# Cosine attention with a highway layer on one core: the k rows of batch 4 are transposed by DMA, and the order of the work is written anew

## The chip, the cores and the metric

The kernel runs on one core of a Trainium2 chip. The metric is the device time of one execution in microseconds (us); less is better. Five engines run side by side, each through its own list of instructions in order: TensorE (PE in the profile, with its weight loads as PEld), VectorE (DVE), ScalarE (ACT), GpSimd (POOL) and SyncE (SP). SP computes nothing; it issues DMAs. POOL and ACT issue some too.

## The reference

Eight batches of twelve heads, 448 rows of 64 numbers. Attention uses normalised q and k, so its scores are cosines; a highway layer follows over the 3584 rows of 768.

```python
q_n = q / (norm(q) + 1e-06)
k_n = k / (norm(k) + 1e-06)
attn = softmax(q_n @ k_n.T / tau)
x = (attn @ v) as rows of 12 * 64            # 3584 x 768
H = maximum(x @ w_h, 0)
T = 1 / (1 + exp(-(x @ w_t + b_t)))
out = T * H + (1 - T) * x
```

q, k, v are 8 x 12 x 448 x 64 float32, w_h and w_t 768 x 768. Products are taken in fp16 with float32 sums.

## The kernel before

**Work and tiles.** Each batch has three groups of four heads; a "group" below is such a set, named by batch and number (4 0 is the first of batch 4). For each group, q and k are loaded (SP loads q, POOL loads k and v), squared on ACT or POOL, summed over 64 columns on DVE (line 439), and turned into a scale by a reciprocal root: Ln and Exp on ACT for batch 0 and a part of batch 1 (lines 465 and 468), seven small DVE steps for later ones (lines 450 to 457). Line 480 multiplies a half of the group by its scale, on POOL or DVE, into the tile qn or kn. Then the group has to be transposed, so that the head's 64 columns lie on the partitions: `turn` (line 484).

**Two ways to transpose.** Either PE does it in seven 128x128 matmuls against an identity (line 496), and DVE copies the result from PSUM to the tile qT or kT (line 499); or one DMA issued by SP does it (line 489). The ranges QDMA and KDMA (line 270) say from which batch on the DMA is used: q from batch 3, k from batch 5. The attention output x is turned by DMA from batch 1 on (line 695, tile xT).

**Scores, softmax, output.** PE multiplies kT and qT (line 506; four matmuls on quarters of the array make two PSUM tiles), ACT takes the exponential (line 538 into E, line 549 into Et for the tail of 64 rows), PE multiplies with v (lines 566 and 574, 65 columns: the 65th gives the row sum), and DVE divides (lines 581 and 582) into x. The highway layer follows per 128 rows: PE (lines 715 and 712; three matmuls make half a sum), DVE adds the bias and takes the products (744, 753, 759, 780), ACT the tanh (757), POOL or DVE the last sum (786), SP stores (793, 796).

**What sets the order.** Nothing is scheduled at run time. `Plan` collects some 1,840 operations, and the table ORDER lists them in the order in which they are put into the engines' lists. SLOTS says which buffer each takes (three kn, three qn, four kT and four qT, eight PSUM banks). ELSEWHERE moves single operations to another engine. BEHIND adds a wait of one operation for another. An engine runs its list in order, so an operation that waits holds up all that stands behind it on its engine. SP's list holds the loads of q, the DMA transposes and the stores in one line. At the start PE runs 43 matmuls on zeros (lines 350 and 354) ahead of and between the first real work.

Of the kernel before, what the change touches and what calls it, by code (L numbers as in the profile page):

```python
# [90 lines left out]
""".split()  # L91
)
SLOTS = {
    "qr": "01010101",
    "kr": "0120121",
    "kn": "012012012012012201021201",
    "vr": "01010110",
    "vp": "01010101",
    "sq": "012012020102102102102102102020202120210102102012",
    "n2": "01010101",  # L100
    "y": "01201201",
    "tu": "01010101010",
# [789 lines left out]
```

## Time and profile before

| | |
|---|---|
| median of three timed runs | 247.79 us (247.62 to 248.25) |
| the profiled execution: its own time | 246.7 us |
| the profiled execution: from first to last instruction (span) | 244.9 us |
| mean granted TensorE clock | 0.991 |
| PE transposes of kn (line 496) | 105 matmuls, 8.3 us busy |
| DMA transposes into kT and qT | 9 and 15 |
| DMA transposes into xT | 28 |

A profile row names a source line, an engine, an operation and the tiles it writes and reads (`out<-in`). A row of the timeline begins with its start and its length in us; in brackets stands the idle time before it and what ended that. Matmuls overlap: one row's length is longer than the distance to the next row's start, and it is the distance that says what an instruction costs on a busy PE. The rows that matter are quoted in the prediction.

### The profile page before, as it was taken

To read this page: it belongs to the slowest core of one execution; us is meant where nothing else is said; L and a number is where in the kernel's file an instruction comes from. 1 tells how busy PE (TensorE), PEld (TensorE's weight loads), DVE (VectorE), ACT (ScalarE), POOL (GpSimd) and SP (SyncE) were. 2 spreads that over 40 slices of the span, in tenths; PEclk is the share of its full clock that TensorE was granted. 3 is DMA by queue.
4 is the path that set the end of the run, shared out by engine and by line. 5 is a ranking of instruction groups with operands and counts; after the bars stand their busy time and mean duration, and the time that the engine had idled before them with its cause. 6 is when DMAs were issued, how large, how long until landed. Compare 5 with 4: busy or idle time off the path is not lost.

```text
span 244.9 us, 8269 instructions
## 1 busy us (share of the span) xinstructions
PE 231.5 (94%) x3304; PEld 143.0 (58%) x3304; DVE 217.4 (89%) x480; ACT 206.3 (84%) x415; POOL 157.9 (64%) x187
## 2 busy tenths in 40 slices
PE   7868899999989999999999999999999999999990
PEld 2334676565765657656664576656565656666550
DVE  4879999999998999999999999899988695768993
ACT  3589999999999999999999999998879787972220
POOL 8596969979983989887676957785665020023340
PEclk9999999999999999999999999999999999999996
DMA  6999999999899969999999899899997647546636
GB/s 224 331 204 265 247 285 225 201 270 226 145 144 235 232 162 230 156 220 220 287 159 202 147 210 212 162 245 197 179 192 156 112 84 148 149 130 130 189 95 155
DMA packets 74647, 47.54 MB, mean 194 GB/s; under 512 B 50288, under 2 KB 71408, under 8 KB 74608
## 3 DMA queue, kind: packets, MB, share of 16 engines
q1 hardware_dynamic: 53776, 32.65, 59.8%
q0 software_dynamic: 19856, 12.68, 39.4%
q10 hardware_dynamic: 976, 1.67, 2.1%
q8 instruction: 26, 0.43, 0.7%
q14 instruction: 13, 0.11, 0.1%
HBM read 38.34 MB, written 11.01 MB: 201 GB/s over the span
## 4 chain that ended last, share of the span: by engine, by line
PE 72%; DVE 10%; ACT 7%; DMA 7%; issue 2%; SPq 1%; DVEq 0%; ACTq 0%
PE B L715 36%; PE B L506 13%; PE B L566 12%; PE B L712 5%; DMA qr<-in_q_dram 4%; ACT E L538 4%; PE B L574 3%; DMA xT<-x 2%; DVE n L439 2%; PE B L496 2%; ACT sq L429 1%; DVE z L744 1%; DVE hm L753 1%; ACT Et L549 1%; DVE qT L499 1%
## 5 line engine op out<-in xcount | busy, mean ns | idle before, releaser
L538 ACT ACTIVATE E<-B 128x448 f16<-128x448 f32 x276 | 135.0, 603 | 9.0 <-PE B L506 6.7
L715 PEld LDWEIGHTS <-xT 128*128 128x128 f16 x576 | 51.2, 98 | 38.7 <-issue 9.6
L786 POOL TENSOR_TENSOR os<-x,hm 128x384 f32<-128x384 f16 x41 | 37.0, 911 | 53.5 <-DVE hm L780 17.4
L715 PE MATMUL B<-wh,xT 128*128 128x384 f16 x288 | 57.2, 326 | 1.0 <-DMA xT<-x 1.0
L715 PE MATMUL B<-wt,xT 128*128 128x384 f16 x288 | 56.3, 326 | 0.1
L439 DVE TENSOR_REDUCE n<-sq 128x14 f32<-128x896 f32 (+1 forms) x50 | 51.0, 1037 | 1.9 <-ACT sq L429 1.7
L506 PE MATMUL B<-qT,kT 64*64 64x448 f16 (+2 forms) x728 | 47.9, 338 | 1.4 <-ACT E L538 0.6
L566 PEld LDWEIGHTS <-E 128*128 128x128 f16 x828 | 38.2, 97 | 10.4 <-issue 5.6
L566 PE MATMUL B<-vp,E 128*128 128x65 f16 x828 | 43.3, 194 | 0.1
L757 ACT ACTIVATE tt<-z 128x768 f16<-128x768 f32 (+1 forms) x32 | 25.9, 810 | 15.5 <-DVE z L744 15.5
L566 PE MATMUL B<-vp,Et 128*128 128x65 f16 x276 | 38.5, 191 | 0.0
L480 POOL TENSOR_TENSOR qn<-qr,y 128x448 f16<-128x448 f32 x38 | 35.0, 935 | 4.5 <-DVE kn L480 1.4
L480 POOL TENSOR_TENSOR kn<-kr,y 128x448 f16<-128x448 f16 x34 | 31.6, 936 | 7.6 <-DVE y L457 2.4
L753 DVE SCALAR_TENSOR_TENSOR hm<-B,x 128x384 f16<-128x384 f32 x53 | 29.0, 551 | 3.9 <-PE B L715 3.5
L744 DVE TENSOR_TENSOR z<-B,bias 128x384 f32<-128x384 f32 x48 | 25.6, 550 | 4.6 <-PE B L715 4.0
L506 PEld LDWEIGHTS <-kT 64*64 64x64 f16 x728 | 17.1, 105 | 20.4 <-issue 15.4
L582 DVE SCALAR_TENSOR_TENSOR x<-B,rd 128x448 f16<-128x448 f32 x46 | 28.0, 617 | 0.7
L566 PEld LDWEIGHTS <-Et 128*128 128x128 f16 x276 | 27.2, 99 | 0.0
L549 ACT ACTIVATE Et<-B 128x448 f16<-128x448 f32 x46 | 26.5, 604 | 0.0
L429 ACT ACTIVATE sq<-qr 128x896 f32<-128x896 f32 (+1 forms) x22 | 22.4, 1018 | 4.6 <-DMA qr<-in_q_dram 4.6
L386 POOL DMA_DIRECT2D vr<-in_v_dram x32 | 22.2, 698 | 5.4 <-DVE vp L511 3.5
L780 DVE TENSOR_TENSOR hm<-tt,hm 128x768 f16<-128x768 f16 (+1 forms) x30 | 15.0, 501 | 0.2
(74 smaller groups left out, 274.4 us busy)
## 6 DMA issues: line engine op xcount, KB each, us to landing
qr<-in_q_dram SPq DMA_DIRECT2D x24, 448.0 KB, 6.8
out_dram<-os SPq DMA_DIRECT2D x47, 192.0 KB, 3.7
kr<-in_k_dram POOLq DMA_DIRECT2D x7, 672.0 KB, 13.8
vr<-in_v_dram POOLq DMA_DIRECT2D x16, 192.0 KB, 10.7
vr<-in_v_dram POOLq DMA_DIRECT2D x16, 144.0 KB, 6.1
out_dram<-os SPq DMA_DIRECT2D x15, 96.0 KB, 3.2
E<-in_k_dram ACTq DMA_DIRECT2D x3, 448.0 KB, 7.5
wt<-in_moe_w_t_dram POOLq DMA_DIRECT2D x1, 1152.0 KB, 23.7
```

The costliest lines, as they stand in the source:

```text
L439: nc.vector.reduce_sum(R("n2", b)[:, c : c + 7 * n], a, axis=AX.X)
L480: ENG[eng].tensor_mul(R(nm + "n", i)[:, :, t, :], source(nm, b, g)[:, t].rearrange("l (j d) -> l j d", d=D), R("y", b)[:, c : c + NJ].unsq ...
L506: nc.tensor.matmul(out[t][64 * h : 64 * h + 64, o[t] : o[t] + w], lhsT=K[ln, j, S_, :], rhs=Q[ln, :, S_, :], start=True, stop=True)
L538: nc.scalar.activation(R("E", n)[:, at : at + 7, :].rearrange("l j x -> l (j x)"), R("B", ("S", n, c, t))[:, 0:S], AF.Exp, scale=1.0 / tau)
L549: op("ACT", f"expt {i} {t}", lambda t=t: nc.scalar.activation(R("Et", (i, t)).rearrange("l j x -> l (j x)"), R("B", ("St", i, t))[:, 0:S], ...
L566: nc.tensor.matmul(U[:, 2 * c + t, :], lhsT=lt.rearrange("l j x -> l (j x)"), rhs=vp[:, 3 * t + m if m < NC else 6 + t, 0:65], start=(m == ...
L582: op("DVE", f"ev {n}", lambda: nc.vector.scalar_tensor_tensor(out=R("x", b)[:, :, D * p : D * p + D], in0=U_()[:, :, 0:D], scalar=0.0, in1 ...
L715: nc.tensor.matmul(P[:, 0:MH], lhsT=xT[:, cc, :], rhs=w_[:, cc, MH * mh : MH * mh + MH], start=(cc == 0), stop=(cc == CC - 1))
L744: op("DVE", f"za {g} {mh}", lambda at=at, sl=sl: nc.vector.tensor_add(R("z", g)[:, sl], R("B", at)[:, 0:MH], biast[:, :] if tail else bias ...
L753: op("DVE", f"hm {g} {mh}", lambda at=at, sl=sl, mh=mh: nc.vector.scalar_tensor_tensor(out=R("hm", g)[:, sl], in0=R("B", at)[:, 0:MH], sca ...
L757: op("ACT", f"th{nb} {g}", lambda: nc.scalar.activation(R("tt", g)[:, 0:W], R("z", g)[:, 0:W], AF.Tanh, scale=0.5), r=[("z", g), ("t0",)], ...
L786: op(e, f"out {g} {mh}", lambda sl=sl, mh=mh, e=e: ENG[e].tensor_add(R("os", g)[:, sl], xpart(mh), R("hm", g)[:, sl]), r=[("gg", g), xk], ...
```

## The change

The one line of logic is the range KDMA. The other four tables (ORDER, SLOTS, BEHIND, ELSEWHERE) are replaced by new ones of the same kind. Three copies and three turns (21 matmuls and their weight loads) leave, three DMA transposes come. Line numbers after the tables are two higher.

```diff
@@ ORDER, SLOTS, BEHIND: other numbers throughout
-1 49 50 4 2 36 51 52 27 57 10 0 53 40 56 7 293 3 30 296 13 24 19 58 32 16 22 55 8 35 300 25 62 64 29 526 5 65 38 66 11
+1 49 50 4 3 42 51 52 30 57 16 0 53 6 56 11 28 296 5 54 18 32 58 26 20 55 9 27 21 526 62 47 25 64 17 63 59 14 293 68 65
...
@@ ELSEWHERE (some of the rows that the text speaks of)
-    "sq1 q 0 0 0": "DVE",
     "sq1 q 0 0 1": "ACT",
-    "sq2 q 0 1 0": "POOL",
-    "qn7 0 0 1": "DVE",
+    "qn7 0 0 0": "POOL",
     "kn7 0 0 0": "POOL",
+    "kn7 0 0 1": "DVE",
-    "kn7 4 0 0": "DVE",
+    "kn7 4 1 0": "DVE",
...
@@ tile_cosine_attention__then__highway_ffn_kernel
-    XDMA, QDMA, KDMA = range(1, B), range(3, B), range(5, B)
+    XDMA, QDMA, KDMA = range(1, B), range(3, B), range(4, B)
```

Three places are shown as the lists of the engines have them. The first is PE's list before, in batch 3's scores, where group 4 2 was turned (kn0 holds its k; seven pairs of line 496, three pairs of line 715 on either side, of which one each is shown):

```order
L715 LDWEIGHTS xT5_113
L715 MATMUL B7_132<-wt_135,xT5_113 128x384
...
L496 LDWEIGHTS kn0_66
L496 MATMUL B1_126<-ident_133,kn0_66 128x128
...
L715 LDWEIGHTS xT2_110
L715 MATMUL B3_128<-wh_134,xT2_110 128x384
```

The same layer of the same rows in PE's list now (xT4 holds what xT5 held before):

```order
L717 LDWEIGHTS xT4_112
L717 MATMUL B6_131<-wt_135,xT4_112 128x384
...
L508 LDWEIGHTS kT2_92
L508 MATMUL B2_127<-qT2_88,kT2_92 64x448
```

No turn stands between the layer and batch 3's next scores any more; the same holds for groups 4 0 and 4 1. Ahead of the first scores of batch 4 PE's list has the same operations as before, less two of the three turns.

The second place is SP's list around batch 4's transposes. Before (q of groups 4 1, 4 0 and 4 2, in this order, go to qT1, qT3 and qT2; `out` rows are stores, `qr` rows loads of batch 6):

```order
L796 DMA out_0_dram<-os0_121 64x768 x2
L489 DMA_TRANSPOSE qT1_87<-qn2_85 128x7x128
L489 DMA_TRANSPOSE qT3_89<-qn1_84 128x7x128
L796 DMA out_0_dram<-os3_124 64x768 x2
L793 DMA out_0_dram<-os1_122 64x384 x2
L373 DMA qr0_61<-in_q_dram 128x2x448
L489 DMA_TRANSPOSE qT2_88<-qn0_83 128x7x128
```

Now (k of groups 4 1, 4 0 and 4 2 goes to kT3, kT0 and kT1; q of groups 4 0, 4 2 and 4 1 to qT3, qT0 and qT1):

```order
L798 DMA out_0_dram<-os0_121 64x768 x2
L491 DMA_TRANSPOSE kT3_93<-kn0_66 128x7x128
L798 DMA out_0_dram<-os1_122 64x768 x2
L491 DMA_TRANSPOSE kT0_90<-kn1_67 128x7x128
L697 DMA_TRANSPOSE xT5_113<-x3_107 128x3x128
L491 DMA_TRANSPOSE qT3_89<-qn2_85 128x7x128
L491 DMA_TRANSPOSE qT0_86<-qn0_83 128x7x128
L375 DMA qr0_61<-in_q_dram 128x2x448
L491 DMA_TRANSPOSE kT1_91<-kn2_68 128x7x128
L795 DMA out_0_dram<-os3_124 64x384 x2
L375 DMA qr0_61<-in_q_dram 128x2x448 x2
L491 DMA_TRANSPOSE qT1_87<-qn1_84 128x7x128
```

The three k transposes stand among those of q, the transpose into qT3 (group 4 0, which is used first) has two k transposes and one of x close ahead of it, and q of group 4 1 went from the first place to the last.

The third place is the start of ACT's list: squares of q and k (line 429), Ln and Exp of the scale (465, 468), and the first exponentials (538). Before, from the first scale on:

```order
L468 ACTIVATE y0_78<-tu0_81 128x28
L429 ACTIVATE sq0_73<-E1_95 128x896
L429 ACTIVATE sq1_74<-qr0_61 128x896
L429 ACTIVATE sq2_75<-qr1_62 128x896
L465 ACTIVATE tu1_82<-n20_76,eps_138 128x28
L468 ACTIVATE y0_78<-tu1_82 128x28
L429 ACTIVATE sq0_73<-E2_96 128x896
L538 ACTIVATE E3_97<-B0_125 128x448
```

Now:

```order
L470 ACTIVATE y0_78<-tu0_81 128x28
L431 ACTIVATE sq2_75<-qr0_61 128x896
L431 ACTIVATE sq0_73<-E1_95 128x896
L431 ACTIVATE sq1_74<-qr0_61 128x896
L467 ACTIVATE tu1_82<-n20_76,eps_138 128x28
L470 ACTIVATE y0_78<-tu1_82 128x28
L431 ACTIVATE sq2_75<-qr1_62 128x896
L431 ACTIVATE sq0_73<-E2_96 128x896
L540 ACTIVATE E3_97<-B0_125 128x448
```

The Ln and Exp of the second group stand ahead of the square of batch 1's q (qr1) instead of behind it, and a square that POOL did before (of q, group 0 1) is on ACT. On POOL and DVE, the halves of the very first group changed places: before DVE scaled both halves of q and POOL both of k; now DVE scales one half of k, and POOL, behind that, half of q, half of k and the other half of q.

More of the change, by code (lines that the diff above doesn't have):

```diff
@@ L95 @@
     "kr": "0120121",
-    "kn": "012012012012012201021201",
+    "kn": "012012012012012012120102",
     "vr": "01010110",
     "vp": "01010101",
-    "sq": "012012020102102102102102102020202120210102102012",
+    "sq": "012012012012210210120120102120020101201012210212",
     "n2": "01010101",
@@ L102 @@
     "tu": "01010101010",
-    "qn": "012012012120120210012021",
-    "qT": "01230123023132031203123",
-    "kT": "01230123012301231023102",
-    "E": "01230123021032310230121032103210321023103213021032110",
-    "Et": "0123012301230123012301230123012301230123012301",
-    "rd": "01001010101010101010101010101011010101010110101010",
-    "x": "012301230",
-    "xT": "01234510234501325403125403152435",
-    "z": "01010101011001010100010101101010",
-    "tt": "01101010110101001010010110110100",
-    "hm": "01202012022110210210210121110210",
@@ L114 @@
-    "os": "01231212031232013012023230213201",
-    "B": (
-        "0123456701234567012345670123456701234567021356402150202730024016735051743571250757647152674036741563"
-        "0274615327405264301526123750467236547026435147356167035406523745136273405217463234567012405673104765"
-        "2014527451026341567024731652074123067124537523641067352431705642160725407321545361027471642501356072"
-        "4570342163104217054635461023754156473150764137426510654271341325470647235173204165720413250614752405"
-        "4063150473672501437560210147632014260375421672315046315426071562154730146725036127541267054160123572"
-        "6034517036427531026745130613247057264305763240162371042365172403517624"
+    "qn": "012012021012201201012102",
@@ new lines @@
+    "qT": "01230123021301231023103",
+    "kT": "01230123012301203102312",
+    "E": "01230120312031320132032012301320123021301321032013230",
+    "Et": "0123021302130202130213021302130213021302130213",
+    "rd": "01010101010101010101010101010101010101010101010101",
+    "x": "012301230",
+    "xT": "01234520134502314503214503214532",
+    "z": "01010101011001001010101010001010",
+    "tt": "01100101010110101010100001010100",
+    "hm": "01221210201020120120102021010210",
+    "os": "01231230131212013103120102301302",
@@ new lines @@
+    "B": (
+        "0123456701234567012345670123456701234567013256407246417417425602414537012041356204576541250764201632"
+        "5746102743601723504761423570452316354216537426307432014576237502467413625704126037514205674203741560"
+        "2716570233105462756341071403526714035627014675204371624753023670154765021347240531432605701574627350"
+        "4173527105467125463025741752064131420652367014530246713716543026312706435217605423642530754362170435"
+        "2053641471603176402317402561027452374016304527615427136057267245036410572657412036412706345103642751"
+        "3627054316750763152467163025476753240635127453726401537246017534621"
@@ L134 @@
 ELSEWHERE = {
-    "sq1 q 0 0 0": "DVE",
     "sq1 q 0 0 1": "ACT",
-    "sq2 q 0 1 0": "POOL",
-    "vt 0 1": "DVE",
-    "qn7 0 0 1": "DVE",
+    "qn7 0 0 0": "POOL",
     "kn7 0 0 0": "POOL",
+    "kn7 0 0 1": "DVE",
     "qn7 0 1 0": "POOL",
@@ L143 @@
     "kn7 0 2 1": "DVE",
+    "out 0 0": "DVE",
+    "out 3 0": "DVE",
     "sq2 k 1 1 0": "POOL",
     "sq2 k 1 2 0": "POOL",
-    "out 6 1": "DVE",
+    "out 7 0": "DVE",
+    "sq2 q 2 0 0": "POOL",
+    "sq2 k 2 1 0": "ACT",
     "sq2 k 2 2 0": "POOL",
+    "vt 2 0": "DVE",
     "kn7 2 0 1": "DVE",
     "out 10 0": "DVE",
-    "vt 3 1": "DVE",
-    "qn7 3 1 0": "DVE",
-    "qn7 3 2 0": "DVE",
-    "kn7 4 0 0": "DVE",
+    "out 10 1": "DVE",
+    "qn7 3 1 1": "DVE",
+    "out 13 1": "DVE",
+    "vt 4 1": "DVE",
+    "kn7 4 1 0": "DVE",
     "qn7 4 2 1": "DVE",
-    "out 16 0": "DVE",
+    "out 17 0": "DVE",
     "out 17 1": "DVE",
-    "out 18 1": "DVE",
-    "qn7 5 0 0": "DVE",
-    "kn7 5 1 1": "DVE",
+    "out 18 0": "DVE",
+    "out 19 0": "DVE",
+    "qn7 5 0 1": "DVE",
+    "qn7 5 1 0": "DVE",
     "out 20 0": "DVE",
-    "out 20 1": "DVE",
     "out 21 1": "DVE",
     "out 22 1": "DVE",
-    "out 23 0": "DVE",
-    "kn7 6 0 0": "DVE",
-    "kn7 6 1 0": "DVE",
-    "qn7 6 2 0": "DVE",
+    "qn7 6 1 1": "DVE",
+    "kn7 6 2 0": "DVE",
     "out 24 1": "DVE",
+    "out 25 1": "DVE",
     "sq2 q 7 0 0": "POOL",
-    "sq2 k 7 1 0": "POOL",
-    "vt 7 0": "DVE",
-    "qn7 7 0 1": "DVE",
-    "kn7 7 0 0": "DVE",
-    "qn7 7 1 1": "DVE",
+    "sq2 q 7 1 0": "POOL",
+    "vt 7 1": "DVE",
+    "qn7 7 0 0": "DVE",
+    "qn7 7 1 0": "DVE",
     "kn7 7 1 0": "DVE",
-    "kn7 7 1 1": "DVE",
-    "out 29 0": "DVE",
+    "qn7 7 2 0": "DVE",
+    "out 29 1": "DVE",
 }
```

148 rows, old and new, of tables (BEHIND, ORDER) are left out of this document.

## Prediction

> **What bounds the kernel now.** First the page: the span, the engines' busy time, and the shares of the chain that ended last.
>
> ```profile
> span 244.9 us, 8269 instructions
> PE 231.5 (94%) x3304; PEld 143.0 (58%) x3304; DVE 217.4 (89%) x480; ACT 206.3 (84%) x415; POOL 157.9 (64%) x187
> PE 72%; DVE 10%; ACT 7%; DMA 7%; issue 2%; SPq 1%; DVEq 0%; ACTq 0%
> ```
>
> PE leads, but three engines are close. An average over the span does not say which of them sets the end, so next the busy time in four stages (columns: stage, length, then busy us of PE, PEld, DVE, ACT, POOL, granted clock, DMA share).
>
> ```profile
> 0.00:36.00 36.00, 30.14 (x403) 16.68 (x407) 29.91 (x67) 28.19 (x58) 27.82 (x37) 1.00 1.12 259
> 36.00:160.00 124.00, 122.84 (x1834) 77.44 (x1826) 119.58 (x260) 122.55 (x244) 100.80 (x118) 1.00 1.15 203
> 160.00:220.00 60.00, 60.00 (x938) 37.61 (x937) 48.23 (x111) 51.14 (x110) 22.11 (x26) 1.00 0.88 158
> 220.00:245.00 25.00, 18.47 (x137) 11.30 (x135) 19.68 (x45) 4.42 (x6) 7.16 (x8) 0.91 0.59 142
> ```
>
> From 36 to 160 PE is idle for 124.00 - 122.84 = 1.16 us and ACT for 1.45. Both are full, and DVE nearly so. From 160 to 220 PE has no idle time, while ACT has 60 - 51.14 = 8.9 us and DVE 11.8. So ACT can be late or early by some us and catch up after 160; PE cannot. **The end is PE's work, plus the time until PE is first fully fed, plus a tail of the last rows.** In the first 36 us PE's busy time holds matmuls on zeros and waits inside matmuls, so it says little there.
>
> **The turns that leave.** Three turns of batch 4, as the timeline of PE shows them, each with the row that follows.
>
> ```profile
> 111.41 0.55 PE L496 MATMUL B<-ident,kn 128*128 128x128 f16 x7
> 111.80 0.26 PE L566 MATMUL B<-vp,E 128*128 128x65 f16 x3
> ...
> 113.88 0.55 PE L496 MATMUL B<-ident,kn 128*128 128x128 f16 x7
> 114.27 0.65 PE L715 MATMUL B<-wh,xT 128*128 128x384 f16 x3
> ...
> 118.24 0.55 PE L496 MATMUL B<-ident,kn 128*128 128x128 f16 x7
> 118.63 0.26 PE L566 MATMUL B<-vp,E 128*128 128x65 f16 x3
> ```
>
> A turn holds PE from its start to the next row's start: 0.39 us, three times. That is 3 x 0.39 = **1.17 us** (by the rows' own lengths, 3 x 0.55 = 1.65 is the most it could be). No bracket stands in these rows, so no wait hides in them. They lie in the stage where PE has no room, and the PE lists hold the same other work ahead of batch 4's first scores, so I take 1.17 in full. What is next behind PE there is ACT; if ACT set the pace, the 1.17 would become idle time of PE. That is a rival below.
>
> The DVE copies behind the turns go too:
>
> ```profile
> 116.96 0.62 DVE L499 COPY kT<-B 128x896 f16<-128x896 f16 x1
> 117.49 0.24 DVE L453 TENSOR_TENSOR tu<-y 128x84 f32<-128x84 f32 x1
> ```
>
> One holds DVE for 0.53 us, so three give 1.6. DVE is not the engine that ends last from 160 on, and I put nothing on this: it is cover for the operations that ELSEWHERE moved to DVE (four more 128x384 sums, fewer scalings).
>
> **The transposes that come.** No k of batch 4 was turned by DMA, but later batches were (first and last start, min/median/max):
>
> ```profile
> L489 SPq DMA_TRANSPOSE kT<-kn x9: 1222/1245/2167, 130.0 to 200.2; - x9
> DMA to landing us min/median/max: 2.9/4.6/6.5
> ...
> L489 SPq DMA_TRANSPOSE qT<-qn x15: 1220/1281/2087, 81.5 to 192.8; - x15
> DMA to landing us min/median/max: 2.9/5.0/7.8
> ```
>
> Each holds SP for 1.24 us, three 3.7, and lands 4.6 us (2.9 to 6.5) after issue, where turn and copy take some 0.55 + 0.62 = 1.2. It costs nothing if k is scaled early enough and SP gets to it. POOL's list now scales the k of group 4 0 fourth among batch 4's halves, with one small copy and one sum between; the start and prices are in these rows.
>
> ```profile
> 101.45 0.94 POOL L480 TENSOR_TENSOR kn<-kr,y 128x448 f16<-128x448 f16 x1 [0.98 <-DVE y L457]
> 102.35 0.91 POOL L786 TENSOR_TENSOR os<-x,hm 128x384 f32<-128x384 f16 x1
> ...
> 111.79 0.50 POOL L523 COPY vp<-vr 64x384 f16<-64x384 f16 x1
> ```
>
> From 101.45 that makes 4 x 0.94 + 0.50 + 0.91 = 5.2, so 106.6. SP then issues kT0, 1.24 us, and it lands between 109.5 and 113.1. PE first needs it at
>
> ```profile
> 115.94 0.38 PE L506 MATMUL B<-qT,kT 64*64 64x448 f16 x4
> ...
> 105.97 4.78 SPq L489 DMA_TRANSPOSE qT<-qn x2
> 114.58 1.24 SPq L489 DMA_TRANSPOSE qT<-qn x1
> ```
>
> less two turns (0.78) and what the start gives (0.48, next part): 114.7. Slack 1.6 us or more: **nothing** for k. The q of the same group is tighter. Its second half is two scalings later, 108.5; ahead of it on SP stand kT0 and a transpose of x, 106.6 + 1.24 + 1.3 = 109.2; it lands at 114.2 with the median, 117.0 with the slowest. Median slack 0.5. I take nothing there as well, and keep 117.0 - 114.7 = 2.3 us as the other end.
>
> The Trainium skill, "VectorE: DVE Perf Modes", sections "The three transpose paths" and "Rules for kernel authors", speaks against the change: TensorE where a PSUM destination will do, at 390 ns per 128x128 against 1309 ns by DMA. This trace does not bear out that price: seven such blocks landed together after 4.6 us, not 7 x 1309 ns = 9.2 us (an estimate from that page), and on PE seven cost 0.39 us together, not 2.7. By the page a group would come 4.6 us later than I have it; that is a rival below.
>
> **The start.** ACT's and PE's rows up to the first exponentials, and what POOL and DVE did for the first group:
>
> ```profile
> 8.67 0.23 ACT L468 ACTIVATE y<-tu 128x28 f32<-128x28 f32 x1
> 8.93 1.86 DVE L480 TENSOR_TENSOR qn<-qr,y 128x448 f16<-128x448 f32 x2 [0.64 <-ACT y L468]
> 10.92 1.83 POOL L480 TENSOR_TENSOR kn<-E,y 128x448 f16<-128x448 f32 x2 [1.15 <-issue]
> 12.81 0.56 PE L496 MATMUL B<-ident,kn 128*128 128x128 f16 x7 [0.97 <-POOL kn L480]
> 13.02 0.95 ACT L429 ACTIVATE sq<-qr 128x896 f32<-128x896 f32 x1 [1.91 <-DMA qr<-in_q_dram]
> 13.87 0.30 ACT L465 ACTIVATE tu<-n,eps 128x28 f32<-128x28 f32 x1
> 14.09 0.75 PE L506 MATMUL B<-x 64*64 64x448 f16 x10 [0.29 <-DVE x L499]
> 14.34 0.93 ACT L429 ACTIVATE sq<-E 128x896 f32<-128x896 f32 x1
> 15.18 2.69 ACT L538 ACTIVATE E<-B 128x448 f16<-128x448 f32 x6
> ```
>
> Before 13.02 ACT idles 1.91 us for a load. The Ln and Exp that ran at 13.87 move into that hole, so the next square starts at 13.86 instead of 14.34 and the exponentials 0.48 earlier, at 14.7. The square that came from POOL (one more of 0.95) fits too. Are scores there by then? DVE's half of k from 8.9 for 0.62, three halves on POOL at 0.93, turn 0.56, copy 0.62, first score 0.4: 8.9 + 0.62 + 2.8 + 0.56 + 0.62 + 0.4 = 13.9. Yes. From there ACT is without idle time, so PE's full stage begins **0.48 us** earlier. Ends: POOL's three halves in a row could be late as easily (a 0.93 us half slipping costs that), so +0.5 to -0.6, the latter if the scores also help.
>
> **The other move.** At 73.80 PE waited for a transpose of x:
>
> ```profile
> 73.80 0.99 PE L715 MATMUL B<-wh,xT 128*128 128x384 f16 x5 [0.96 <-DMA xT<-x]
> ```
>
> It is the one long wait in PE's full stage. Now the load of q that SP issued behind those transposes stands ahead of them, but four v loads were brought to about that time, and PE has the same work to fill the wait with. I take 0; ends: the wait is gone (-0.96) or a us longer. The tail has the same operations in nearly the same order: 0.
>
> **Sum.** -1.17 - 0.48 = -1.65: span 244.9 to 243.25, the profiled execution's own 246.7 to 245.05. The median of the runs lies 1.1 above that execution, so I take the same step from it: 247.79 - 1.65 = **246.1 us**.
>
> **Rivals.**
> - *ACT sets the pace through 160, and the turns become idle time of PE.* For it: ACT idle only 1.45 us in 124. Against: ACT's 8.9 us after 160. Then only the start counts: 247.3. Chance 0.20.
> - *The transpose into qT of group 4 0 comes late* (slower). SP's list is in order; what stands ahead of it waits for POOL and holds it up, and the slowest landing stalls PE 2.3 us: 246.1 + 2.3 = 248.4; with 0.3 us more of waiting for POOL's halves, 248.7. It decides from a landing at 114.7 + 1.65 + 0.74 = 117.1. For it: DMA share over 1 in that stage. Against: four v loads left it, and the median is in time. Chance 0.15.
> - *Transposes cost a group 4.6 us more* (the skill's price). kT0 would land at 106.6 + 4.6 + 4.6 = 115.8 and qT3 at 118.8, PE stalls 4.1: 250.2. Against: 24 landings in this trace with medians under 5.1. Chance 0.03.
> - *The wait at 73.80 goes too*: 246.1 - 0.96 = 245.1. Chance 0.12.
>
> **Chances.** The forecast has 0.50. About 0.3%, 0.74 us, is what a measurement of this kernel can tell from no change. Faster by more: 0.50 + 0.12 = 0.62. Within: 0.20. Slower: 0.15 + 0.03 = 0.18. The range goes from 244.9 (wait gone and the start's better end) to 248.4 (the slow rival's first price); it leaves out the slow ends.
>
> **What would show it.** Right: no L496 rows on kn after 100 us; PE busy all but 1 us from 36 to 160; the first exponential at 14.7; batch 4's first score near 114.7 without a bracket; PE's last rows 1.65 earlier. Wrong: a bracket on PE that names DMA qT or kT near 115 (second rival); as much idle time on PE as the turns took, ended by ACT (first); a longer wait than 0.96 at the first layer of batch 1; POOL late in the first 13 us.

## The result, and the profile after

The changed kernel takes **245.53 us** (median of four runs, 245.1 to 245.97) against 247.83 for the kernel before in the same runs: ratio 0.9918, 95% interval 0.989 to 0.9945, that is 2.0 us less (1.4 to 2.7). Forecast were 246.1 us and a step of 1.65. A second set of runs gave 245.13 against 247.27, ratio 0.9916 (0.9892 to 0.994). Ratios leave disturbed runs out, medians do not; where they differ below, the ratio counts.

The page of the kernel after: span, busy times and the chain's shares.

```profile
span 243.6 us, 8257 instructions
PE 230.5 (95%) x3283; PEld 141.8 (58%) x3283; DVE 214.9 (88%) x476; ACT 207.4 (85%) x417; POOL 156.7 (64%) x186
PE 73%; ACT 13%; DMA 8%; issue 2%; DVE 2%; DVEq 0%; ACTq 0%
```

ACT's share of the chain went from 7 to 13%. The four stages, with one more row for 88 to 116 us, where batch 4's turns were prepared (columns as above):

```profile
0.00:36.00 36.00, 30.12 (x399) 17.05 (x399) 27.75 (x63) 29.35 (x60) 27.47 (x38) 1.00 1.10 260
36.00:160.00 124.00, 122.86 (x1831) 75.80 (x1827) 119.79 (x262) 122.85 (x246) 97.74 (x113) 1.00 1.17 208
160.00:220.00 60.00, 60.00 (x932) 38.21 (x929) 49.18 (x113) 51.18 (x109) 25.14 (x31) 1.00 0.92 163
220.00:245.00 25.00, 17.54 (x132) 10.75 (x129) 18.22 (x41) 4.04 (x6) 6.31 (x7) 0.94 0.53 130
...
88.00:116.00 28.00, 27.90 (x398) 16.66 (x398) 27.56 (x58) 27.95 (x57) 22.18 (x24) 1.00 1.03 189
```

PE is as full as before up to 220; what it saved shows in the last row, 17.54 us against 18.47. In 88 to 116 ACT has 0.05 us without work. The same stretch before:

```profile
88.00:116.00 28.00, 28.00 (x426) 17.85 (x422) 27.83 (x62) 27.97 (x57) 24.49 (x28) 1.00 1.20 205
```

ACT was full there then, too. The DMA share fell from 1.20 to 1.03 although transposes were added: POOL issued five v loads in this stretch before and issues one now.

What was said of batch 4, from the groups of PE and the timelines of SP and PE in the kernel after:

```profile
L498 PE MATMUL B<-ident,kn 128*128 128x128 f16 x84 | 6.7, 219 | 0.3 <-POOL kn L482 0.2
...
104.62 1.23 SPq L491 DMA_TRANSPOSE kT<-kn  x1
...
107.23 1.29 SPq L491 DMA_TRANSPOSE kT<-kn  x1
108.57 1.41 SPq L697 DMA_TRANSPOSE xT<-x  x1
110.23 3.23 SPq L491 DMA_TRANSPOSE qT<-qn  x2
113.58 0.51 SPq L375 DMA_DIRECT2D qr<-in_q_dram  x1
114.21 1.24 SPq L491 DMA_TRANSPOSE kT<-kn  x1
...
115.83 0.57 PE L508 MATMUL B<-qT,kT 64*64 64x448 f16 x8
```

21 matmuls are gone. The k of group 4 0 is issued at 107.23 (forecast 106.6), its q at 110.23, and no bracket stands at batch 4's first score. That score is the second half of the last row; it starts at 116.04.

### The profile page after: what moved, and what is told of

It reads as the page before. It is cut to its first block, busy times and chain, and to the rows that moved or that the text cites. A ratio compares the mean times of both kernels' runs of the same rounds, so it can differ in the third digit from the quotient of the medians.

```text
span 243.6 us, 8257 instructions
## 1 busy us (share of the span) xinstructions
PE 230.5 (95%) x3283; PEld 141.8 (58%) x3283; DVE 214.9 (88%) x476; ACT 207.4 (85%) x417; POOL 156.7 (64%) x186
## 4 chain that ended last, share of the span: by engine, by line
PE 73%; ACT 13%; DMA 8%; issue 2%; DVE 2%; DVEq 0%; ACTq 0%
PE B L717 36%; PE B L508 13%; PE B L568 13%; ACT E L540 9%; PE B L714 5%; DMA qr<-in_q_dram 3%; PE B L576 3%; DMA xT<-x 2%; PE B L498 2%; DMA E<-in_k_dram 2%; ACT sq L431 2%; ACT Et L551 1%; ACT tt L759 1%; PE B L640 1%; ACT E L626 1%
## 5 line engine op out<-in xcount | busy, mean ns | idle before, releaser
L788 POOL TENSOR_TENSOR os<-x,hm 128x384 f32<-128x384 f16 x37 | 33.3, 912 | 46.1 <-DVE hm L782 19.4
L508 PE MATMUL B<-qT,kT 64*64 64x448 f16 (+2 forms) x728 | 48.5, 338 | 2.0 <-ACT E L540 0.5
L482 POOL TENSOR_TENSOR qn<-qr,y 128x448 f16<-128x448 f32 x39 | 35.9, 935 | 14.2 <-DVE rd L583 5.5
L482 POOL TENSOR_TENSOR kn<-kr,y 128x448 f16<-128x448 f16 x38 | 35.2, 934 | 11.9 <-DVE y L459 7.4
L568 PE MATMUL B<-vp,E 128*128 128x65 f16 x828 | 41.9, 194 | 0.6 <-issue 0.5
L568 PEld LDWEIGHTS <-E 128*128 128x128 f16 x828 | 37.5, 97 | 8.3 <-issue 4.3
L568 PE MATMUL B<-vp,Et 128*128 128x65 f16 x276 | 37.8, 191 | 0.0
L508 PEld LDWEIGHTS <-kT 64*64 64x64 f16 x728 | 17.9, 105 | 22.6 <-issue 17.3
L551 ACT ACTIVATE Et<-B 128x448 f16<-128x448 f32 x46 | 25.8, 614 | 0.6 <-PE B L508 0.5
L431 ACT ACTIVATE sq<-kr 128x896 f32<-128x896 f16 x15 | 15.8, 1077 | 0.0
```

The source lines that it names most:

```text
L431: nc.scalar.activation(dst, src, AF.Square)
L482: ENG[eng].tensor_mul(R(nm + "n", i)[:, :, t, :], source(nm, b, g)[:, t].rearrange("l (j d) -> l j d", d=D), R("y", b)[:, c : c + NJ].unsq ...
L508: nc.tensor.matmul(out[t][64 * h : 64 * h + 64, o[t] : o[t] + w], lhsT=K[ln, j, S_, :], rhs=Q[ln, :, S_, :], start=True, stop=True)
L551: op("ACT", f"expt {i} {t}", lambda t=t: nc.scalar.activation(R("Et", (i, t)).rearrange("l j x -> l (j x)"), R("B", ("St", i, t))[:, 0:S], ...
L568: nc.tensor.matmul(U[:, 2 * c + t, :], lhsT=lt.rearrange("l j x -> l (j x)"), rhs=vp[:, 3 * t + m if m < NC else 6 + t, 0:65], start=(m == ...
L788: op(e, f"out {g} {mh}", lambda sl=sl, mh=mh, e=e: ENG[e].tensor_add(R("os", g)[:, sl], xpart(mh), R("hm", g)[:, sl]), r=[("gg", g), xk], ...
```

## The experiments

Several kernels below are spliced: OLD and NEW are the orders before and after as lists of operations, and an operation keeps the engine and the added waits of the order it comes from. The buffers do not come along. They are handed out anew: in e2_start 605 of the 1,088 assignments differ from those in the order that the operation comes from, 469 of them PSUM banks; in e10_tail it is 18. So a splice changes more than the order.

**Noise.** The kernel before once more:

> The kernel before once more, unchanged, for a second trace and for the size of the noise. Its first profiled execution took 246.7 us, 1.1 below the median of its timed runs. If that was chance, this profiled execution lies within 0.5 us of the timed median (247.8) and its trace shows where the 1.1 us were; if executions with a profile are always shorter, it lies about 1 us below the timed runs again. The ratio of the timed runs should be 1.000 within 0.002.

247.64 against 247.26 for the others of its kind, ratio 1.0001 (0.9977 to 1.0024). Its profiled execution has a span of 246.5, 1.6 us more than the first trace. ACT's start and PE's long wait in it:

```profile
13.40 0.95 ACT L429 ACTIVATE sq<-qr 128x896 f32<-128x896 f32 x1 [2.28 <-DMA qr<-in_q_dram]
...
75.36 0.82 PE L715 MATMUL B<-wh,xT 128*128 128x384 f16 x4 [1.45 <-DMA xT<-x]
```

A load came 0.4 later and the wait for xT was 0.5 longer; up to that row the second trace is 1.56 us later than the first (73.80), and it stays so to the end. So a trace is good to about 1.5 us in its first 74 us. Behind that these two agree within 0.1 us, and the two traces of the kernel after (next) within 0.4. The first trace was an early one.

The kernel after once more:

> The kernel after once more, unchanged, on the same chip as the three others. Its first timing gave -2.3 us (ratio 0.9918, 0.989 to 0.9945); the two traces differ by 1.3 us in span. If the gain is the turns alone (1.17 us) and the rest was chance in before's start, -1.2 us (0.995). If start and order bring something beside the turns, -2 us (0.992).

Ratio 0.9916; span 243.1, against 243.6. The gain is not that of the turns alone.

**What the turns cost on PE.**

```diff
@@ mm, the layer's matmuls, of the kernel after
                     P, xT = R("B", at), R("xT", g)
+                    if lo == 0 and at[1:] in ((9, 1, 0), (8, 1, 1), (10, 0, 0)):
+                        for j in range(NJ):
+                            nc.tensor.transpose(P.bitcast(FP16)[:, 128 * j : 128 * j + 128], ident[:, :], ident[:, :])
```

> The kernel after with the three DMA transposes left as they are, and PE given back only the work of the three turns: seven 128x128 transposes of the identity ahead of the first matmul of three half sums of the layer, at 108, 113 and 115 us, into the bank that the half sum then overwrites. No wait, copy or buffer is added. Forecast's theory (PE has no room there, so 21 transposes cost 3 x 0.39): 1.17 us more than the kernel after. Rival (ACT sets the pace, PE's share would be idle time): 0 to 0.3 us more.

246.04, ratio 0.9939 (0.9915 to 0.9962): 0.9 more than the kernel after by the medians, 0.6 by the ratios, with 0.1 to 1.2 as an estimate from the scatter of the two sets of runs. PE's timeline of this kernel, two of the three added turns and batch 4's first score:

```profile
108.06 0.55 PE L713 MATMUL B<-ident 128*128 128x128 f16 x7
...
115.43 0.55 PE L713 MATMUL B<-ident 128*128 128x128 f16 x7
...
116.89 0.57 PE L508 MATMUL B<-qT,kT 64*64 64x448 f16 x8
```

The chain that ended last in the kernel after, about the first of these places:

```profile
105.17 2.88 ACT E L540 x6
...
108.10 2.11 PE B L717 x12
```

It runs over ACT until 108.06 and over PE from 108.10, and the added work stands behind that point, as the turns did before. Start times of single traces can't be compared here (see the noise), but distances within a trace can. From the row of scores just ahead of the first added turn (107.27 here, 107.32 and 106.39 in the two traces of the kernel after) to the score row 9.62 us pass here and 8.51 and 8.50 there: 1.11 more, or 0.37 a turn. From the same row to PE's last layer row it is 130.05 against 129.06 and 129.49, 0.6 to 1.0 more. So PE's work counts in full where the turns stood, and the rival in which it turns into idle time is not borne out there. The timed runs alone would not exclude it (0 to 0.3 us was its price). Of the stretch ahead of 108 us, where ACT is on the chain, this run says nothing.

**The transposes without the new order.**

```diff
@@ SP's list of the kernel before: xd7 transposes, st stores, ldq loads of q
 xd7q 4 0
+xd7k 4 0
 st 2
 st 7
-ldq 6 2
+xd7k 4 2
+xd7k 4 1
 xd7q 4 2
+ldq 6 2
@@ PE's and DVE's lists
-tk 4 0, cpk 4 0, tk 4 2, cpk 4 2, tk 4 1, cpk 4 1
```

> The kernel before with nothing but batch 4's three turns and copies taken out and three DMA transposes put into SP's list: into kT of group 4 0 behind the scaling that ends at 111.1 us, those of groups 4 2 and 4 1 behind the store at 112.1 to 113.8, ahead of the transpose into qT of group 4 2 and the loads of q. Scalings, loads and order are otherwise those of before. If the turns are worth 1.17 us by themselves: -1.2 us (0.995). If they need the earlier scalings and v loads of the new order: kT of group 4 0 is issued at 111.1, PE wants it at 115.2; a landing of 4.6 us gives a wait of 0.5 us and -0.7 us; a landing of 6 to 8 us, as transposes have where the DMA engines are backed up, a wait of 2 to 4 us on DMA kT and 1 to 3 us more than before.

Ratio **1.0124** (1.0075 to 1.0173): 3 us slower than before, with the same turns gone. The six runs spread from 248.83 to 254.23 us; the ratio rests on the two shortest, and by the median of all six (252.81) the loss is 5.7. The trace is of the shortest run. SP, then ACT and PE in it:

```profile
111.05 1.23 SPq L491 DMA_TRANSPOSE kT<-kn  x1
112.33 1.22 SPq L798 DMA_DIRECT2D out_dram<-os  x2
113.59 1.71 SPq L795 DMA_DIRECT2D out_dram<-os  x2
115.42 3.17 SPq L491 DMA_TRANSPOSE kT<-kn  x2
118.70 1.31 SPq L491 DMA_TRANSPOSE qT<-qn  x1
120.11 1.04 SPq L375 DMA_DIRECT2D qr<-in_q_dram  x2
...
124.72 0.95 ACT L431 ACTIVATE sq<-qr 128x896 f32<-128x896 f32 x1 [2.96 <-DMA qr<-in_q_dram]
...
126.15 1.68 PE L508 MATMUL B<-qT,kT 64*64 64x448 f16 x8 [1.82 <-ACT E L540]
```

kT was nearly in time: it landed at 115.80, 4.75 us after its issue, and batch 4's first score waits 0.3 us until 115.84 (the profile puts that wait down to ACT). By the expectation such a landing meant 0.7 us less than before; the loss that came has the size of its third case, but not its cause. From that score to PE's last layer row 124.10 us pass, against 121.37 in the first trace of before, although one turn less stands there. The loss is behind the score: the three transposes take 4.4 us of SP's time, the load of q behind them goes out at 120.11 instead of 113.96, ACT's list has that load's square ahead of the next exponentials and waits 2.96 us, and PE waits for the exponentials. The place of that load was chosen for this run; with it ahead, a transpose of group 4 1 or 4 2 would have been later instead, which was not tried. In the kernel after the same load leaves at 113.58, because two of the transposes were issued by 108.5, and that because their k is scaled earlier. **In the new order SP has room for the transposes; in the old one, placed as here, they cost more than the turns gave.** That no place in the old order would do is not shown.

**The start.**

```diff
-ORDER = OLD
+ORDER = [n for n in NEW if n in OLD[:260]] + OLD[260:]
```

> The order of the kernel after for the first 36 us (260 operations), the order of the kernel before from there on; batch 4's k is transposed on PE and copied by DVE. Forecast's theory (the start is worth 0.48 us because ACT's exponentials begin earlier): -0.5 us against before, PE's work from 36 us on 0.5 earlier. Rival (the earlier exponentials are lost again before 36 us, as the lag of PE behind its own work in the two traces suggests, 23.5 us at 36 us in both): 0.0 us. Bound between them: -0.25 us.

Ratio 1.0017 (1.0 to 1.0033): no gain. The reverse:

```diff
-ORDER = NEW
+ORDER = [n for n in OLD if n in NEW[:260]] + NEW[260:]
```

> The kernel after with the first 36 us (260 operations) in the order and on the engines of the kernel before; the reverse of e2_start. Forecast's theory (start worth 0.48 us): 0.5 us more than the kernel after (ratio to before 0.9935). Rival (start worth nothing, as e2_start's 1.0017 says): 0.0 us against the kernel after (0.9916). If e2_start's +0.4 us is real and the old start is the better one: 0.4 us less than the kernel after (0.990).

Ratio 0.9955 (0.9932 to 0.9979), 1.0 us more than the kernel after. But the seam costs something of its own:

```profile
37.87 0.56 PE L498 MATMUL B<-ident,kn 128*128 128x128 f16 x7 [0.66 <-POOL kn L482]
```

The wait stands just behind the seam; the kernel after has none there. The two runs do not agree on the start. The second is not clean, and both have other buffers than the kernels that they come from.

**The tail.**

```diff
-ORDER = OLD
+ORDER = [n for n in OLD if n in NEW[:1780]] + NEW[1780:]
```

> The kernel before up to 221 us, its last 59 operations (the layers of the last three blocks of rows, their sums and stores) in the order of the kernel after; k of batch 4 on PE. In four traces with the old tail 7.1 to 7.3 us lie between PE's last matmul and the end of the span, in five with the new one 6.7 to 6.8. If the order of the tail does that: 0.4 us less than before (0.998) and 6.7 to 6.8 us in the trace. Forecast's theory (tail 0): 1.000 and 7.1.

Ratio 1.0021 (0.9999 to 1.0042), no gain, and the trace keeps the long tail: the last layer row starts at 237.32 of a span of 245.1. The order of the last operations is not what shortens it.

**Cuts elsewhere, and what their seams cost.** The new order to 95 us, then the old:

```diff
-ORDER = OLD
+ORDER = [n for n in NEW if n in OLD[:740]] + OLD[740:]
```

> The order of the kernel after for the first 95 us, that of the kernel before from there on; batch 4's k is transposed on PE and copied by DVE. Forecast's theory (start 0.48, nothing between 36 and 95 us): -0.5 us. Rival one (nothing before batch 4): 0.0 us. Rival two (the order ahead of 95 us holds most of the gain): -1.5 to -2 us.

Ratio 1.004 (1.0019 to 1.0062), slower. The old order to 95 us, and to 72 us, then the new:

```diff
-ORDER = NEW
+ORDER = [n for n in OLD if n in NEW[:740]] + NEW[740:]
```

> The order of the kernel before for the first 95 us (740 operations), the order of the kernel after from there on; batch 4's k is transposed by DMA. Forecast's theory (1.17 us of turns): -1.2 us against before. Rival one (all of the measured 2.3 us comes from batch 4 on, turns and order together): -2.3 us. Rival two (the turns became idle time that ACT ends, and the order ahead of 95 us brought the gain): -0.3 us or less.

Ratio 1.0224 (1.0194 to 1.0254). What both orders had ahead of the cut at different places was squeezed against it. POOL, PE and DVE in its trace:

```profile
96.25 2.01 POOL L388 DMA_DIRECT2D vr<-in_v_dram  x3
98.25 0.97 POOL L482 TENSOR_TENSOR kn<-kr,y 128x448 f16<-128x448 f16 x1
...
99.27 0.56 PE L498 MATMUL B<-ident,kn 128*128 128x128 f16 x7 [0.90 <-POOL kn L482]
...
103.86 0.46 DVE L513 COPY vp<-vr 128x1152 f16<-128x1152 f16 x1 [5.97 <-DMA vr<-in_v_dram]
...
106.25 1.05 PE L508 MATMUL B<-qT,kT 64*64 64x448 f16 x4 [4.15 <-DVE kT L501]
```

Three load issues of v, 2.0 us, stand ahead of one scaling on POOL: that makes the wait of 0.90 us on PE. The wait of 4.15 us has the same loads behind it, but another way: DVE's list has a copy of the loaded v ahead of the copy into kT, DVE waits 5.97 us for those late loads, and the copy into kT starts at 105.59 although its turn was done by 99.8.

```diff
-ORDER = NEW
+ORDER = [n for n in OLD if n in NEW[:560]] + NEW[560:]
```

> The order of the kernel before for the first 72 us (560 operations), that of the kernel after from there on, k of batch 4 by DMA; cut earlier than e3_late, where the v loads that the kernel after issues at 74 to 77 us had been squeezed into POOL's list at 93 to 98 us and held up the last scaling of batch 3's k. Forecast's theory (turns only): -1.2 us against before. If the order from 72 us on brings something of its own: -2 us or more. If the first 72 us held the gain: 0 us.

Ratio 1.0068 (1.0043 to 1.0092); here PE waits 2.4 us:

```profile
63.90 2.99 DVE L513 COPY vp<-vr 128x1152 f16<-128x1152 f16 x1
...
69.38 0.91 PE L508 MATMUL B<-qT,kT 64*64 64x448 f16 x8 [2.38 <-DVE x L584]
```

The copy of v stands ahead of the seam on DVE; it took 2.99 us, where the longest other copy of this form in the fourteen traces took 0.83. Why is not shown, so this wait is not known to be the seam's. Neither late cut says how much of the gain lies behind it. They say that the halves of two orders, each good as a whole, did not add here.

**Further in the same direction.** Batch 3's k by DMA, in the new order:

```diff
-    XDMA, QDMA, KDMA = range(1, B), range(3, B), range(4, B)
+    XDMA, QDMA, KDMA = range(1, B), range(3, B), range(3, B)
```

> The kernel after with batch 3's k transposed by DMA as well: three turns (21 matmuls) and three DVE copies leave, three DMA transposes join SP's list behind the scalings that they read, nothing else moves. If a turn of PE's full stage is worth its 0.39 us wherever a transfer is in time: 1.17 us less than the kernel after. If ACT sets the pace between 82 and 98 us: 0 to -0.3 us. If SP or the DMA engines bring kT late (group 3 2 is scaled last, 96.5 us, first scores at 107; group 3 1 at 90.6, first scores at 97.1): a wait on PE named DMA kT, +0.5 us or more.

Ratio 1.0259 (1.0217 to 1.0301). SP and PE:

```profile
84.95 8.63 SPq L491 DMA_TRANSPOSE qT<-qn  x2
...
94.95 2.06 SPq L491 DMA_TRANSPOSE kT<-kn  x1
...
98.44 4.46 SPq L491 DMA_TRANSPOSE kT<-kn  x1
...
102.68 1.34 PE L508 MATMUL B<-qT,kT 64*64 64x448 f16 x12 [6.57 <-DMA kT<-kn]
```

The k of group 3 1 was scaled at 89.5 and issued at 94.95, behind a store and two transposes that held SP for 8.63 us. In the kernel after the same two took:

```profile
86.10 5.28 SPq L491 DMA_TRANSPOSE qT<-qn  x2
```

That is already more than twice the usual 1.22 us each. The wait of 6.57 us is not the whole loss: behind it TensorE's granted clock is 0.66 between 100 and 110 us (last section). Then two groups of batch 3 only, with that transpose ahead of the store:

```diff
-        if b in (QDMA if nm == "q" else KDMA):
+        if b in (QDMA if nm == "q" else KDMA) or (nm, b) == ("k", 3) and g < 2:
```

> The kernel after with two of batch 3's three groups of k (3 0 and 3 1) transposed by DMA too, the third left on PE; unlike e8_k3_by_dma, the scaling of group 3 1 stands 1.9 us earlier in POOL's list, its transpose ahead of a store, and one load of q behind it. If the transfers are in time, two turns leave: -0.8 us against the kernel after (0.9885 against before). If SP is held in its issues as in e8_k3_by_dma (transposes of 3.5 to 5 us on SP instead of 1.24): PE waits for DMA kT of 3 1 at 96 us, 0 to +3 us against the kernel after.

Ratio 1.0105 (1.0071 to 1.0139). PE's waits for DMA:

```profile
97.25 0.76 PE L508 MATMUL B<-qT,kT 64*64 64x448 f16 x12 [0.64 <-DMA kT<-kn]
...
103.92 0.66 PE L717 MATMUL B<-wt,xT 128*128 128x384 f16 x3 [2.96 <-DMA xT<-x]
```

kT was now nearly in time, and the transposes of x behind it on SP late. No version beat the kernel after.

## Why the prediction was right, point by point

Time, sign and range held. The terms did not all hold, and that the step came within 0.4 us (2.0 by the ratio, against 1.65) is in part luck: in the table below the first part gave 0.4 less than forecast, the second 0.4 more, and the tail, forecast at 0, gave 0.5. (The range's lower end adds up to 245.0, 246.1 - 0.96 - 0.12, and not to 244.9; nothing hangs on it.) The terms are best read at two rows that stand in both kernels. Ahead of batch 4's first score PE's list has the same operations but for two turns, and behind PE's last layer row (line 728, now 730) only the tail is left. The last layer row in the kernel before and after:

```profile
237.31 1.16 PE L728 MATMUL B<-wh,xT 128*64 128x192 f16 x24
```

```profile
236.38 1.16 PE L730 MATMUL B<-wh,xT 128*64 128x192 f16 x24
```

| part | forecast | before (three traces) | after (two traces) | measured |
|---|---|---|---|---|
| start to batch 4's first score | -0.78 - 0.48 = -1.26 | 115.94, 117.50, 115.89 | 116.04, 115.10 | -0.87 |
| from there to the last layer row | -0.39 | 121.37, 121.31, 121.43 | 120.34, 120.78 | -0.81 |
| from there to the end of the span | 0 | 7.59, 7.69, 7.78 | 7.22, 7.22 | -0.47 |
| sum | -1.65 | | | -2.15 |

(Means against means. The third trace of before is e10_tail, the kernel before up to 221 us; the score in the trace of e5_after_again is again the second half of its row.) The sum agrees with the 2.0 and 2.1 us of the timed runs.

- **The turns, 1.17: right in kind, a little large at the end.** By e6_turns_back PE's part is 1.11 at batch 4's first score, and 0.6 to 1.0 at the end by ratio, medians and traces.
- **k by DMA costs nothing: right in this order only.** The scaling of kT0's last half ended at 106.8 (forecast 106.6), and the landings were in the forecast windows: no bracket at 115.83. The rival of a late transpose did not occur, but e11_turns_alone shows how near it was, in another form: not qT late, but a load behind the transposes on SP. The prediction counted the three issues of 1.24 us and priced them at nothing without naming what stands behind them; in the new order that holds, since SP's list has room for them.
- **The start, 0.48: its step failed in one trace, its worth stays open.** The exponentials did begin earlier:

```profile
12.22 0.23 ACT L470 ACTIVATE y<-tu 128x28 f32<-128x28 f32 x1
13.13 0.95 ACT L431 ACTIVATE sq<-qr 128x896 f32<-128x896 f32 x1 [0.69 <-DMA qr<-in_q_dram]
...
14.82 1.39 ACT L540 ACTIVATE E<-B 128x448 f16<-128x448 f32 x3
...
35.10 1.47 ACT L626 ACTIVATE E<-B 128x512 f16<-128x512 f32 x3 [0.50 <-PE B L508]
```

  14.82 against 15.18, and ACT's wait for the load shrank from 1.91 to 0.69. But the step "from there ACT is without idle time, so PE's full stage begins 0.48 earlier" does not hold in this trace: ACT waits 0.50 us for PE at 35.10, more than the 0.36 that it had gained, where the kernel before has no such wait. e2_start has the same rows, with 0.51 at 35.03, and is not faster. The second trace of the kernel after has the early exponentials (14.92) and no such wait. What the table shows for the first part (-0.87, less than the turns and the start together) rests on three traces that scatter by 1.6 us and two that differ by 0.9; how much of it is the start stays open.
- **ACT as the pace: true for a stretch, not for the end.** Between 88 and 116 us ACT is full and the chain runs through it until 108.06, and batch 4's first score came at 116.04 in the first trace, not at 114.7. From there to the last layer row the new order gave 0.42 more than the one turn left. That length is 121.3 to 121.4 us in five traces with the old order behind that point and 120.2 to 120.8 in six with the new one (e8_k3_by_dma and e12_two_groups_of_3 left aside), the turn included, so it goes with the order; which rows of it, no run separated.
- **The wait for xT: right at 0, within the scatter.** It is 1.02 in the first trace of after and 0.35 in the second, against 0.96 and 1.45 in the two of before and 0.46 in e10_tail (there put down to DVE):

```profile
74.22 1.15 PE L717 MATMUL B<-wt,xT 128*128 128x384 f16 x6 [1.02 <-DMA xT<-x]
```

- **The tail, 0: wrong by 0.4 to 0.5.** See the last section.
- **The price of the rival by rate** did not show: batch 4's k transposes landed 3.9 to 4.8 us after issue. The Trainium skill ("VectorE: DVE Perf Modes", "The three transpose paths") would give 9.2 us for seven blocks, an estimate from its time for one block, which this trace does not bear out.

## What to carry to other kernels

Work taken off a full engine and given to a DMA is not free of queues: count what the issuing engine holds for each transfer, and name the first thing behind it that another in-order list waits for. Here the kernel became 2 us faster with the whole order rebuilt around the replacement, and 3 us or more slower with the replacement alone, in the one place tried. A piece cut out of an order that was searched as a whole tells little about the piece; adding the suspected work back into the finished kernel told more.

## What had not been expected of the hardware

**A DMA transpose can hold SP far longer than its usual 1.22 us.** In e8_k3_by_dma (least, median and longest ns of one):

```profile
L491 SPq DMA_TRANSPOSE qT<-qn x15: 1221/1300/5034, 80.4 to 201.0; - x15
L491 SPq DMA_TRANSPOSE kT<-kn x15: 1222/1506/4462, 81.8 to 197.8; - x15
```

The longest lie between 85 and 103 us, where loads of q, k and v are in flight and the DMA share is 1.2 to 1.3; that the backlog is the cause was not tested by itself.

**TensorE's granted clock fell behind some long waits of PE.** In the kernel after it is 1.00 from 88 to 116 us. It is 0.66 from 100 to 110 us in e8_k3_by_dma (wait of 6.57 us), 0.75 from 100 to 110 in e3_late (4.15) and 0.83 from 70 to 80 in e7_late2 (2.38), but 1.00 from 90 to 120 in e12_two_groups_of_3 (2.96) and from 110 to 140 in e11_turns_alone (1.82). At the lower clock the same work is slower: three matmuls of the layer that begin at 108.63 in e3_late hold PE for 0.94 us, to the start of the next row, where they hold it for 0.49 in the kernel after (108.58 to 109.07). So such a wait can cost more than its own length; the length from which it does can't be read from these five runs.

**Program code and the last stores.** The page counts the transfers that bring instructions: 26 in the kernel before, 25 in the kernel after (row q8, packets and MB).

```profile
q8 instruction: 26, 0.43, 0.7%
```

```profile
q8 instruction: 25, 0.41, 0.7%
```

In each of the five traces with the long tail (7.6 to 7.8 us behind the start of the last layer row) one such packet falls between 237 and 241 us, and the store issued then holds SP longer; the other nine have none there and tails of 7.0 to 7.2. Before and after:

```profile
237.58 1.54 SPq L796 DMA_DIRECT2D out_dram<-os  x2
```

```profile
236.62 1.11 SPq L798 DMA_DIRECT2D out_dram<-os  x2
```

e10_tail (new order at the end, 26 packets) has 1.54 and the long tail; e11_turns_alone (old order, 25 packets) the short one; e6_turns_back has 26, the last of them between 232 and 237 us, and the short one. So the 0.47 us goes with that packet, which comes and goes with the 42 instructions of the turns on PE, and not with the order of the tail. It was not tried by itself.
